# Decode attention over a long cache: VectorE passes PE's marks to the load queue by event instructions, and two loops are loaded at other slots

## The chip, the cores and the metric

The kernel runs on one core of one Trainium2 chip. The metric is the device time of one execution in microseconds (us), the median of three runs. Engines are PE (TensorE, matmul), VectorE (DVE), ScalarE (ACT), GpSimd (POOL) and SyncE (SP, which here only issues DMAs).

## The reference

One token's hidden vector `x` (512 numbers) goes through a layer norm. On the result run, side by side, an attention block with a cache and a small two-layer network; both are added to `x`.

```python
xn = _layernorm(x)
q = (xn @ wq).reshape(1, 1, 32, 128).transpose(0, 2, 1, 3)      # 32 query heads of 128
k, v = repeat(k_cache, 4), repeat(v_cache, 4)                   # 8 key/value heads, 65536 keys each
scores = einsum("bhqd,bhkd->bhqk", q, k) * 128 ** -0.5
o = einsum("bhqk,bhkd->bhqd", softmax(scores), v)
out = x + o.reshape(1, 1, 4096) @ wo + maximum(xn @ w1, 0) @ w2
```

All numbers are float32. The caches k and v hold 8 x 65536 x 128 numbers each: 268 MB for k, the same for v, read once.

## The kernel before, in words

Each of the 8 key/value heads is cut into five blocks (`PART = [7, 7, 6, 6, 6]`, in units of 2048 keys, here called tiles). That makes 40 steps (`STEPS`). There is one buffer for k (`ks`) and one for v (`vs`), each as large as the largest block, 7 tiles. A load of a block of 7 tiles is 7168 KB, of 6 tiles 6144 KB. SP issues them in turn: k, v, k, v, and so on (lines 152 to 161). Before each k load it waits until the semaphore `k_free` has counted the steps so far, before each v load the same of `v_free`. After the last step it waits for `k_free` once more, and then loads `w1` and `w2` into `ks` and `wo` into another buffer (lines 162 to 166 and 268 to 283).

A step runs as follows.

- PE (loop at line 300) waits for the k load and multiplies each of `MOST` = 7 tiles of `ks` with the current queries, four matmuls a tile (line 307). The results go in turn to two PSUM buffers, `pa` and `pb`, two tiles each. After each pair of tiles, and after the last single one, PE adds one to the semaphore `s_tiles`: it reaches 1, 2, 3 and 4 in a step. PE always works on 7 tiles; in a block of 6 the last is old data that is not used.
- VectorE (loop at line 332, one iteration a head, five blocks written out in it) waits for each mark of `s_tiles` and transposes the pair into `tr` (line 336). Then it takes 4 off `s_tiles` (line 342). A `drain` (line 343) waits until its work so far is done, and adds one to `k_free`. Then come the maximum over the block (lines 345 to 348), with PE's help the maximum over partitions (lines 350 to 353), and the bias for the exponential.
- ScalarE (loop at line 377) takes the exponentials into `wt` (line 384) and the factor `alpha` by which older sums shrink (line 390).
- PE waits for the v load, multiplies `wt` with `vs` in 56 matmuls (line 323) and adds one to `s_o`.
- VectorE waits for `s_o` and merges PE's result into `acc` (line 357 in a head's first block, line 360 in the others). The instruction that merges adds one to `v_free` when it is done.

GpSimd (lines 286 to 297) copies the next head's queries to `qcur` when `k_free` says that the last block of the head has been read. After the loops come the small network, the sums over heads and the output projection (lines 400 to 472).

The argument `head_slot` of a loop (lines 300, 332 and 377) names, for an engine, the instruction slot at which the loop's first instruction is loaded. PE's, VectorE's and ScalarE's loops all have 0. In the built program VectorE's loop has 93 instructions and ScalarE's 34.

Of the kernel before, what the change touches and what calls it, by code (L numbers as in the profile page):

```python
# [13 lines left out]
ENG = mybir.EngineType  # L14
# [3 lines left out]
HQ, HKV, DH = 32, 8, 128  # L18
# [10 lines left out]
PART = [7, 7, 6, 6, 6]  # L29
MOST = max(PART)  # L30
NP = len(PART)
# [37 lines left out]
def attention_and_mlp_kernel(  # L69
# [22 lines left out]
    nc = tc.nc  # L92
    scale = float(DH) ** -0.5
    te, ve, se, ge, sy = nc.tensor, nc.vector, nc.scalar, nc.gpsimd, nc.sync
# [35 lines left out]
    acc_o, acc_z, acc_y, pm = (ps.tile([P, 512], F32, name=n) for n in ("acc_o", "acc_z", "acc_y", "pm"))  # L130

    names = "k_in v_in tiles scores m_out bias_out a_out w_out o_out k_free v_free q_in d_out f_out f_free"
    with tc.tile_critical():
# [18 lines left out]
        for i in range(STEPS):  # L152
            h, n = divmod(i, NP)
# [69 lines left out]
        s = DV.mark  # L223
# [76 lines left out]
        with nc.Fori(0, STEPS, engines=[ENG.PE], head_slot={ENG.PE: 0}):  # L300
            te.wait_ge(k_in, 16).then_inc(k_in, -16)
            te.wait_ge(q_in, 1).then_inc(q_in, -1)  # L302
            for s in range(MOST):
                pt = (pa, pb)[s // 2 % 2][:, s % 2, :]
                for c in range(CT):
                    at = (s * CT + c) * TW
                    i = te.matmul(pt[32 * c : 32 * c + 32, :], qcur, ks[:, at : at + TW], start=True, stop=True)  # L307
# [12 lines left out]
            n = MOST * SUB // WIDE  # L320
# [8 lines left out]
            mm.then_inc(s_o, 1)  # L329


        with nc.Fori(0, HKV, engines=[ENG.DVE], head_slot={ENG.DVE: 0}):
            for n, nt in enumerate(PART):
                for s in range(0, MOST, 2):
                    w = min(2, MOST - s)
                    i = ve.transpose(  # L336
                        tr[:, s * SUB : (s + w) * SUB, :].rearrange("p b i -> p (b i)"),
                        (pa, pb)[s // 2 % 2][:, :w, :].rearrange("p i k -> p (i k)"),
                    )._wait_ge(s_tiles, s // 2 + 1)
                    if s < 4:  # L340
                        i.then_inc(s_dve, 1)
                ve.sem_inc(s_tiles, -4)
                ve.drain().then_inc(k_free, 1)  # L343
                top = m if n == 0 else mc
                i = ve.reduce_max(top, tr[:, : nt * SUB, :G].rearrange("p b g -> p g b"), axis=AX.X)  # L345
                if n:
                    ve.drain()
                    i = ve.tensor_max(m, m, mc)  # L348
                i.then_inc(s_dve, 1)
                ve.reduce_max(mg, pm[:G, :P], axis=AX.X)._wait_ge(s_max, 1)  # L350
                ve.drain()
                ve.tensor_scalar(dg, idg, mg, -scale, op0=ALU.mult, op1=ALU.mult).then_inc(s_dve, 1)  # L352
                ve.tensor_copy(bias[:, n, :], pm[:, P : P + G + 1])._wait_ge(s_max, 2).then_inc(s_bias, 1)  # L353
                ve.sem_inc(s_max, -2)
                flat = acc.rearrange("p b d -> p (b d)")
                if n == 0:
                    i = ve.tensor_copy(flat, acc_o)  # L357
                else:
                    ve.wait_ge(s_alpha, 1).then_inc(s_alpha, -1)
                    i = ve.scalar_tensor_tensor(  # L360
                        flat, flat, alpha[:, n : n + 1], acc_o, op0=ALU.mult, op1=ALU.add
                    )
                i._wait_ge(s_o, 1).then_inc(v_free, 1)
                ve.sem_inc(s_o, -1)
            ve.drain()
            last = bias[:, NP - 1, :G].unsqueeze(1).to_broadcast([P, NP - 1, G])
            ve.tensor_sub(diff, last, bias[:, : NP - 1, :G]).then_inc(s_diff, 1)
            ve.tensor_mul(masked, acc, selb.unsqueeze(2).to_broadcast([P, WIDE, DH]))
            ve.wait_ge(s_alpha, 1).then_inc(s_alpha, -1)
            ve.tensor_mul(part[:, : NP - 1, :], part[:, : NP - 1, :], fac)  # L370
            ve.wait_ge(f_free, 1).then_inc(f_free, -1)
            ve.drain()
            ve.reduce_sum(fin[:, DH:], part.rearrange("p n g -> p g n"), axis=AX.X)
            ve.reduce_sum(fin[:, :DH], masked.rearrange("p b d -> p d b"), axis=AX.X).then_inc(f_out, 1)


        with nc.Fori(0, HKV, engines=[ENG.Activation], head_slot={ENG.Activation: 0}):
            for n, nt in enumerate(PART):
                se.wait_ge(s_bias, 1).then_inc(s_bias, -1)  # L379
                if n and nt < PART[n - 1]:  # L380
                    b = slice(nt * SUB, PART[n - 1] * SUB)
                    se.copy(wt[:, b, :].rearrange("p b g -> p (b g)"), zero)  # L382
                for g in range(G):
                    i = se.activation(  # L384
                        wt[:, : nt * SUB, g], tr[:, : nt * SUB, g], AF.Exp, bias=bias[:, n, g : g + 1],
                        scale=scale, accum_out=part[:, n, g : g + 1],
                    )
                i.then_inc(s_w, 1)
                if n:
                    se.activation(  # L390
                        alpha[:, n : n + 1], bias[:, n - 1, G : G + 1], AF.Exp,
                        bias=bias[:, n, G : G + 1], scale=-1.0,
                    ).then_inc(s_alpha, 1)
            se.wait_ge(s_diff, 1).then_inc(s_diff, -1)
            se.activation(
                fac.rearrange("p n g -> p (n g)"), diff.rearrange("p n g -> p (n g)"), AF.Exp
            ).then_inc(s_alpha, 1)
# [104 lines left out]
```

## Time and profile before

| what | value |
|---|---|
| three runs | 1307.83, 1311.38, 1313.49 us; median 1311.38 |
| the profiled execution | 1308.58 us, its span (first to last instruction) 1306.8 us |
| granted PE clock, mean | 0.735 of full speed |
| busy share of the span | PE 57%, VectorE 23%, ScalarE 7% |
| read from HBM | 560.99 MB, 429 GB/s over the span |
| PE, k matmuls (line 307) | 359.4 us busy in 2240 instructions |
| PE, v matmuls (line 323) | 328.5 us busy in 2240 instructions |
| VectorE, transposes (line 336) | 176.9 us busy, 1.25 us each for a pair of tiles |
| k load of 6 tiles, issue to landing | median 19.8 us |
| v load of 6 tiles, issue to landing | median 19.4 us |

The profile comes from one execution; all durations below are its own. A landing is told by 16 marks, one from each DMA engine, as each load is cut into equal parts for the 16 engines. An instruction packet is a DMA by which an engine's program is brought in; they have queues of their own.

### The profile page before, as it was taken

The page shows a single profiled execution, that of the slowest core. Times are in us where ns is not written, and L with a number is a line of the kernel's source. Part 1 is how long each engine was busy: PE and PEld are TensorE (multiplying, and loading weights), DVE is VectorE, ACT ScalarE, POOL GpSimd, SP SyncE. Part 2 cuts the span into 40 slices and gives each one's busy share as a digit, 9 for nine tenths or more (in the row PEclk, how much of TensorE's full clock was granted, in tenths as well). Part 3 has the DMA queues.
Part 4 walks back from the last instruction along what each step waited for, and adds up shares of the span by engine and source line. Part 5 has one row for each costly group of instructions (what it writes and reads, how often), then busy time and mean ns, then how long its engine had stood idle before and what let it go on. Part 6 is the DMA issues. An engine that isn't in the chain of part 4 may idle for free. (4 is left out here: it accounts for less than half of the span.)

```text
span 1306.8 us, 11612 instructions
## 1 busy us (share of the span) xinstructions
PE 748.4 (57%) x4958; PEld 214.8 (16%) x4958; DVE 294.9 (23%) x474; ACT 88.3 (7%) x372; POOL 4.6 (0%) x22
## 2 busy tenths in 40 slices
PE   4456555556555655556655655556655656555666
PEld 1111111111111111111111111111111111111112
DVE  2122222222212222222222222222221232222221
ACT  0000000000000001000000000000000000100000
POOL 0000000000000000000000000000000000000000
PEclk9667777777767777777766777777766777777778
DMA  9999999999999999999999999999999999999998
GB/s 397 446 427 412 429 433 437 430 427 432 433 435 432 432 436 432 435 429 433 428 441 432 433 433 428 441 425 433 433 435 441 425 433 437 429 442 429 432 425 353
DMA packets 14408, 561.09 MB, mean 429 GB/s; under 512 B 1592, under 2 KB 1600, under 8 KB 1984
## 3 DMA queue, kind: packets, MB, share of 16 engines
q1 hardware_dynamic: 14248, 561.00, 99.6%
q8 instruction: 3, 0.05, 0.0%
q14 instruction: 5, 0.04, 0.0%
q10 hardware_dynamic: 152, 0.00, 0.0%
HBM read 560.99 MB, written 0.00 MB: 429 GB/s over the span
## 5 line engine op out<-in xcount | busy, mean ns | idle before, releaser
L323 PE MATMUL acc_o<-vs,wt 128*16 128x512 f32 x2240 | 328.5, 750 | 128.6 <-PEq L319 128.6
L307 PE MATMUL pa<-ks,qcur 128*32 128x512 f32 x1280 | 220.1, 820 | 285.8 <-PEq L302 285.8
L336 DVE STREAM_TRANSPOSE tr<-pa 128x1024 f32<-128x1024 f32 x80 | 100.0, 1250 | 404.2 <-PE pa L307 404.2
L307 PE MATMUL pb<-ks,qcur 128*32 128x512 f32 x960 | 139.3, 685 | 0.0
L323 PEld LDWEIGHTS acc_o<-vs,wt 128*16 128x16 f32 x2240 | 76.4, 114 | 347.2 <-issue 347.2
L384 ACT ACTIVATE wt<-tr,bias 128x96 f32<-128x96 f32 (+1 forms) x160 | 73.1, 465 | 875.5 <-ACTq L379 875.5
L307 PEld LDWEIGHTS pa<-ks,qcur 128*32 128x32 f32 x1280 | 48.6, 134 | 420.0 <-issue 409.1
L360 DVE SCALAR_TENSOR_TENSOR acc<-acc,alpha,acc_o 128x512 f32<-128x512 f32 x32 | 23.9, 747 | 348.8 <-PE acc_o L323 348.8
L336 DVE STREAM_TRANSPOSE tr<-pb 128x1024 f32<-128x1024 f32 x80 | 76.9, 962 | 38.0 <-PE pb L307 38.0
L312 PE MATMUL pm<-ident,m 128*4 128x128 f32 x40 | 11.5, 286 | 90.0 <-DVE m L348 73.0
L307 PEld LDWEIGHTS pb<-ks,qcur 128*32 128x32 f32 x960 | 41.2, 138 | 110.5 <-issue 86.6
L313 PE MATMUL pm<-dg,ones 4*128 4x4 f32 x80 | 21.6, 338 | 26.7 <-DVE dg L352 26.7
L384 ACT ACTIVATION_READ_ACCUMULATOR wt<-tr,bias 128x1 f32 x160 | 29.9, 187 | 0.0
L357 DVE COPY acc<-acc_o 128x512 f32<-128x512 f32 x8 | 5.5, 691 | 102.9 <-PE acc_o L323 102.9
L345 DVE TENSOR_REDUCE mc<-tr 128x4 f32<-128x384 f32 (+1 forms) x32 | 26.2, 819 | 3.7
L312 PEld LDWEIGHTS pm<-ident,m 128*4 128x4 f32 x40 | 3.3, 81 | 126.3 <-DVE m L348 102.0
L313 PEld LDWEIGHTS pm<-dg,ones 4*128 4x128 f32 x80 | 18.1, 280 | 34.9 <-DVE dg L352 34.9
L314 PE MATMUL pm<-dg,rowg 4*128 4x1 f32 x80 | 21.6, 337 | 0.0
L314 PEld LDWEIGHTS pm<-dg,rowg 4*128 4x128 f32 x80 | 20.6, 313 | 0.0
L382 ACT COPY wt<-zero 128x64 f32<-128x64 f32 x8 | 2.0, 244 | 232.5 <-ACTq L379 232.5
L242 PE MATMUL pa<-big,xn 128*1 128x512 f32 x64 | 11.5, 888 | 10.0 <-DMA big<-wq 10.0
L353 DVE COPY bias<-pm 128x5 f32<-128x5 f32 x40 | 6.5, 164 | 41.5 <-PE pm L314 41.5
(83 smaller groups left out, 115.3 us busy)
## 6 DMA issues: line engine op xcount, KB each, us to landing
ks<-k SPq DMA_DIRECT2D x24, 6144.0 KB, 19.8
vs<-v SPq DMA_DIRECT2D x24, 6144.0 KB, 19.4
ks<-k SPq DMA_DIRECT2D x16, 7168.0 KB, 23.5
vs<-v SPq DMA_DIRECT2D x16, 7168.0 KB, 24.3
big<-wq SPq DMA_DIRECT2D x2, 4096.0 KB, 17.2
ks<-w SPq DMA_DIRECT2D x2, 3584.0 KB, 17.7
big<-wo SPq DMA_DIRECT2D x1, 4096.0 KB, 31.4
big<-wo SPq DMA_DIRECT2D x1, 2048.0 KB, 35.9
```

The source lines that it names most:

```text
L242: lambda e: e.matmul(pr[32 * c : 32 * c + 1, :n], xn[:, a : a + 1], weights(c, a), start=(a == 0), stop=(a == A - 1),),
L307: i = te.matmul(pt[32 * c : 32 * c + 32, :], qcur, ks[:, at : at + TW], start=True, stop=True)
L312: te.transpose(pm[:G, :P], m, ident)._wait_ge(s_dve, 3).then_inc(s_max, 1)
L313: te.matmul(pm[:, P : P + G], ones[:G, :], dg[:, :G], start=True, stop=True)._wait_ge(s_dve, 4)
L314: te.matmul(pm[:, P + G : P + G + 1], rowg, dg[:, G : G + 1], start=True, stop=True).then_inc(s_max, 1)
L323: mm = te.matmul(acc_o[32 * c : 32 * c + WIDE * G, :], wt[:, i * WIDE : (i + 1) * WIDE, :].rearrange("p b g -> p (b g)"), vs[:, i * 512 : ...
L336: i = ve.transpose(tr[:, s * SUB : (s + w) * SUB, :].rearrange("p b i -> p (b i)"), (pa, pb)[s // 2 % 2][:, :w, :].rearrange("p i k -> p ( ...
L345: i = ve.reduce_max(top, tr[:, : nt * SUB, :G].rearrange("p b g -> p g b"), axis=AX.X)
L353: ve.tensor_copy(bias[:, n, :], pm[:, P : P + G + 1])._wait_ge(s_max, 2).then_inc(s_bias, 1)
L357: i = ve.tensor_copy(flat, acc_o)
L360: i = ve.scalar_tensor_tensor(flat, flat, alpha[:, n : n + 1], acc_o, op0=ALU.mult, op1=ALU.add)
L384: i = se.activation(wt[:, : nt * SUB, g], tr[:, : nt * SUB, g], AF.Exp, bias=bias[:, n, g : g + 1], scale=scale, accum_out=part[:, n, g : ...
```

## The change

Three edits.

- `k_free` no longer goes up with the drain behind all four transposes. VectorE's program instead has an event instruction that waits for a mark of `s_tiles` and adds one to `k_free`. Which mark depends on how many tiles the next k load will overwrite (`follow`). If the next block has 7 tiles, it is the fourth mark, and the event stands ahead of the last transpose. If the next has 6 tiles, it is the third mark, and the event stands right behind the third transpose. The drain stays, without the addition.
- `v_free` no longer goes up when the merge into `acc` is done. An event instruction ahead of the merge waits for `s_o` and adds one to `v_free`. The wait for `s_alpha` stands ahead of it; the merge itself waits for nothing more.
- The loop of VectorE is loaded from slot 128 and that of ScalarE from slot 68. PE's stays at 0. VectorE's loop now has 103 instructions.

```diff
-        with nc.Fori(0, HKV, engines=[ENG.DVE], head_slot={ENG.DVE: 0}):
+        with nc.Fori(0, HKV, engines=[ENG.DVE], head_slot={ENG.DVE: 128}):
             for n, nt in enumerate(PART):
+
+                follow = PART[(n + 1) % NP]
                 for s in range(0, MOST, 2):
                     w = min(2, MOST - s)
+                    if s < follow <= s + 2 and follow == MOST:
+                        ve.wait_ge(s_tiles, s // 2 + 1).then_inc(k_free, 1)
                     i = ve.transpose(
...
                     if s < 4:
                         i.then_inc(s_dve, 1)
+                    if s < follow <= s + 2 and follow < MOST:
+                        ve.wait_ge(s_tiles, s // 2 + 1).then_inc(k_free, 1)
                 ve.sem_inc(s_tiles, -4)
-                ve.drain().then_inc(k_free, 1)
+                ve.drain()
...
                 flat = acc.rearrange("p b d -> p (b d)")
+                if n:
+                    ve.wait_ge(s_alpha, 1).then_inc(s_alpha, -1)
+                ve.wait_ge(s_o, 1).then_inc(v_free, 1)
                 if n == 0:
-                    i = ve.tensor_copy(flat, acc_o)
+                    ve.tensor_copy(flat, acc_o)
                 else:
-                    ve.wait_ge(s_alpha, 1).then_inc(s_alpha, -1)
-                    i = ve.scalar_tensor_tensor(
+                    ve.scalar_tensor_tensor(
                         flat, flat, alpha[:, n : n + 1], acc_o, op0=ALU.mult, op1=ALU.add
                     )
-                i._wait_ge(s_o, 1).then_inc(v_free, 1)
                 ve.sem_inc(s_o, -1)
...
-        with nc.Fori(0, HKV, engines=[ENG.Activation], head_slot={ENG.Activation: 0}):
+        with nc.Fori(0, HKV, engines=[ENG.Activation], head_slot={ENG.Activation: 68}):
```

## The prediction

> **What bounds the kernel now.** I read the DMA queues first, because the page's slices give the DMA engines a 9 in nearly every slice while PE stands at 5. Then I read the load queue's own waits, one block of the timeline, four stretches, and the trace's records of single DMA packets and landing marks.
>
> From the page of the kernel before (queue: packets, MB, share of the 16 engines' span):
>
> ```profile
> ## 3 DMA queue, kind: packets, MB, share of 16 engines
> q1 hardware_dynamic: 14248, 561.00, 99.6%
> q8 instruction: 3, 0.05, 0.0%
> q14 instruction: 5, 0.04, 0.0%
> ```
>
> The one queue that carries k and v fills the DMA engines for 99.6% of the span. Keep the eight instruction packets in mind; they return below.
>
> What the load queue waits for (total us, times, longest):
>
> ```profile
> SPq L158 <- DVEq L343: 632.4, 39, 49.0
> SPq L161 <- DVE acc L360: 454.0, 31, 16.4
> SPq L161 <- DVE acc L357: 130.6, 8, 16.3
> ```
>
> SP stands in these waits for 1217 of 1306.8 us, and all are on VectorE, as the change supposes. But SP is only the issuer: while it waits for one buffer, the other buffer's load is still in the queue. That shows in a block of the timeline (start, duration):
>
> ```profile
> 329.36 1.04 PE L307 MATMUL pb<-ks,qcur 128*32 128x512 f32 x8
> 329.61 1.25 DVE L336 STREAM_TRANSPOSE tr<-pa 128x1024 f32<-128x1024 f32 x1 [0.47 <-PE pa L307]
> 330.79 0.67 DVE L336 STREAM_TRANSPOSE tr<-pb 128x512 f32<-128x512 f32 x1
> 331.51 0.33 SPq L158 DMA_DIRECT2D ks<-k  x1
> ...
> 344.92 0.75 DVE L360 SCALAR_TENSOR_TENSOR acc<-acc,alpha,acc_o 128x512 f32<-128x512 f32 x1 [10.11 <-PE acc_o L323]
> 345.69 0.33 SPq L161 DMA_DIRECT2D vs<-v  x1
> ```
>
> The k load of 331.51 is issued while v is still moving: v's 16 landing marks come at 334.52 to 335.94. The v load of 345.69 finds k in flight until 351.48. I call the time from an issue to the other load's first mark the **lead**: 3.0 and 5.8 us here; over the 78 issues after the first pair the median is 3.9, the smallest 2.05. In steady state a transfer of 6 tiles lands every 14.53 us, one of 7 every 16.95, whichever engine is how late.
>
> The exceptions are few (stretch, its us, busy us of each engine, granted clock, DMA share, GB/s):
>
> ```profile
> core 0: us, PE busy (x) PEld busy (x) DVE busy (x) ACT busy (x) POOL busy (x), PEclk, DMA share, GB/s
> 23.40:42.45 19.05, 5.65 (x36) 1.27 (x36) 0.86 (x2) 0.00 (x0) 0.19 (x1) 0.68 1.00 427
> 104.00:124.00 20.00, 10.48 (x69) 3.56 (x73) 5.96 (x9) 2.20 (x10) 0.00 (x0) 0.69 0.99 413
> 147.00:165.00 18.00, 9.18 (x61) 2.90 (x61) 2.51 (x7) 2.05 (x9) 0.00 (x0) 0.75 1.00 423
> 500.00:1000.00 500.00, 283.82 (x1872) 81.09 (x1872) 114.84 (x175) 34.18 (x147) 1.74 (x7) 0.72 1.00 433
> ```
>
> 433 GB/s is the plateau; the stretches at 104 and 147 lie below it. There the leads were short (2.45 and 2.61, then 2.05 us), and packets of 49152 bytes, 1.82 us each elsewhere, took up to 3.7. Long packets of the later k and v loads sit nearly all at leads under 2.8 us, which 8 of the 78 issues have. So a queue fed too late costs something, but seldom.
>
> [...]
>
> **The change part by part.**
>
> 1. *k_free.* Before, it goes up with the drain behind the last transpose (331.50). After, an event instruction sends it. Event instructions do not wait for VectorE's running work: the one of line 342 ran at 330.49, inside the transpose of 329.61 to 330.86, and took 0.02 us. For a next load of 7 tiles (2 of 5 blocks) the signal goes with PE's last pair, marked at 330.45: 1.0 us earlier. For one of 6 tiles (3 of 5) it goes with the third pair, marked at 329.59 in this block: 1.85 us earlier. If an event did wait for the transpose, the latter would be 0.6 us.
>
> 2. *v_free.* Today it goes up when the 0.75 us of line 360 end, after the change when PE's mark arrives (344.89): 0.77 us earlier.
>
> 3. *What that is worth.* On the plateau nothing: the earlier load only waits longer in its queue. At the short leads, the 2.05 becomes about 3.9 and the 2.45 about 3.2, above 2.8. What those stalls cost the end is not their packet time summed over engines but what the latest engine's mark lost: 0.06, 0.10 and 0.26 us at steps 2 to 4, nothing clear later. I take **-0.4**, between 0 and -0.65 (the last with all shortfalls of transfer rates counted).
>
> 4. *Ten more event instructions a head on VectorE,* 80 x 0.02 = 1.7 us over 1300, 0.04 a block. Behind them wait a transpose, or the merge of acc; both already wait for the same mark. Cover is the lead of 3.9 us; without it, 1.7 us. SP's issues number the same, nothing is moved past another in its queue, and GpSimd's wait for k_free at a head's end is met 1.0 us earlier. I take 0.
>
> 5. *The slots.* No time of a loop shows before's slots, but the packets do. VectorE's copy of line 262 ends at 30.33 and releases PE, ACT and itself into their loops. At 35.25, 35.27 and 35.33 an instruction packet (8192, 16384, 8192 bytes) goes in ahead of load packets, at 41.16 and 43.16 two more of 8192. The load packets right behind took 3.36, 3.27, 2.60, 2.49 and 2.78 us where 2.12 is usual. Of wq's 16 marks all lie within 0.45 us. Of v's first load, 13 lie within 0.45, the others at 1.62, 2.39 and 2.55. So fetches made three DMA engines late, and every load is cut evenly over 16, so its last mark is that of the latest. The 16384-byte packet with what follows it costs 1.126 + 0.48 = 1.61: that is the mark at 1.62. I take it for PE's, whose slot stays, because its queue and size differ from the rest. The two pairs of 8192 I put to ACT and VectorE, whose heads move from slot 0 to 68 and 128. [...] If both pairs go, the latest mark falls from 2.55 to 1.62: **-0.9**. Bounds: 0 if either pair stays on its engine, and +1.6 if one fetch more hits the latest engine (0.33 + 1.24, the dearest of the 8192). I take -0.9, since all rows fit it.
>
> [...]
>
> 6. *The tail.* PE's fetch at 1287.81 makes one engine late by 1.1 + 0.46 us. In before it hit the engine that led: the spread of marks stayed at 1.3. Where it hits after the change is unknown: 0 to +1.5, as PE's engine of 35.27 may be the latest then. I take 0, as in before.
>
> Sum: the profiled execution took 1308.58 (span 1306.8, 1.8 around it); 1308.58 - 0.9 - 0.4 = **1307.3 us**. The three runs shown are 1307.83, 1311.38 and 1313.49: the profile stands with the lowest, 2.8 below the median. The forecast says that after the change the median, too, lies near the floor. That holds if the excess of the higher runs comes from short leads, as when PE's phases last longer: a k phase now takes 8.9 to 10.5 us from landing to next issue, against a pace of 14.53.
>
> **The rivals.**
>
> - *The queue is never empty, so no wait that goes was on the path, and the higher runs have another cause* (slower packets, say). For it: the plateau of 433 over 500 us, 70 of 78 leads above 2.8. Then the median moves by at most the sum: 1311.4 - 1.3 = 1310.1, up to 1311.4. Chance 0.30.
> - *Slower: the moved loop is fetched again at each of its back edges.* Place: VectorE's loop, now 103 instructions from slot 128. If its start and end do not stay loaded together, seven back edges each put 8192 bytes ahead of loads on one DMA engine, 1.56 us each by the dearest row: 10.9 us of lateness, 1308.2 + 10.9 = 1319.1. It passes 1317.9 (0.5% over the median) only when all seven are fetched again. [...] Chance 0.06, and 0.02 for anything else that slows.
> - *It does not do what it says:* the event waits for the running transpose. Signals come 0.6 us earlier at most; the slots are left: about 1307.7. Chance 0.05.
> - *Faster than a half per cent:* all engines even and no stall. The packets at their usual durations sum to 1295.3 us an engine; with 2.1 ahead, 4.4 behind and 1.8 outside, 1303.6. Chance 0.07.
> - The forecast, 1306.0 to 1309.0: 0.50.
>
> **How the numbers follow.** A measurement of this kernel can tell about 0.5% from no change, which is 6.6 us. Faster is 0.07, slower 0.08, the rest 0.85. From 1305.0 to 1312.5 the range holds the forecast, the first rival and the third, 0.85 together less some of their tails; the unknown fetches (+1.6, +1.5) stay inside.
>
> **What would show it.** In the profile after: leads of at least 3 us; no slice but the first and the last under 425 GB/s (one of 412 before); two or fewer instruction packets on q14 before 100 us; the first k load's marks within 1.7 us; SP's waits as long in total as now, put down to other lines. Wrong, if the early fetches are all there (then 1308.2), or if q14 counts seven more (the slower rival). If issues come earlier and the median stays at 1311, the first rival holds.

## The result, and the profile after

The changed kernel takes 1307.9 us (median of 11 runs, 1306.8 to 1309.1), the kernel before 1310.05 us in the same measurement (11 runs, 1307.8 to 1313.7). The ratio is 0.9979, with a 95% interval of 0.9969 to 0.9988: 2.7 us gained, 1.6 to 4.1 by the interval; the two medians lie 2.15 us apart. Not only the median fell; the runs scatter over 2.3 us instead of 5.9 (those of the kernel before in the three later sets over 3.2, 3.3 and 6.3). The same kernel in a later set of runs, named `change_again` below, gave 0.9988 (0.9978 to 0.9997). Half a per cent, which was set as the bound to "no change", is not reached. The ratios leave out two runs far off the others of their kernel, one of before at 1349.12 us (beside `change_again`) and one of `split_loads` at 2223.9 us.

The profiled execution of the change took 1309.12 us (span 1307.2), the slowest of its 11 runs, while that of before, with 1308.58, lies below 10 of the 11 runs of before. Two single executions therefore do not show the gain as a difference of spans. It has to be read inside them.

The instruction queues on the page after (queue: packets, MB, share of the 16 engines' span):

```profile
q1 hardware_dynamic: 14248, 561.00, 99.5%
q8 instruction: 3, 0.05, 0.0%
q14 instruction: 4, 0.03, 0.0%
```

One packet fewer than before on q14 within the span. The trace's packets say which: of 35.25, 35.33, 41.16 and 43.16 us before, 35.13, 35.32 and 43.45 are still there. The slots took one fetch away and not four.

What the load queue waits for, after (total us, times, longest):

```profile
SPq L161 <- DVEq L364: 617.4, 39, 17.5
SPq L158 <- DVEq L347: 338.4, 24, 15.8
SPq L158 <- DVEq L339: 259.4, 15, 47.0
```

The waits add up to 1215.2 us, where they were 1217.0. They have only gone over to the new event instructions: line 364 for v, 347 for a next load of 6 tiles (24 times), 339 for one of 7 (15 times). A reader who expected a shorter wait would think that nothing had happened. The wait did not shrink, as the loads set the pace (q1 took 99.5% of the 16 engines' span, 99.6% before). What moved is when, within the pace, an issue falls. The block of the timeline that the prediction showed, now (start, duration):

```profile
328.61 1.25 DVE L340 STREAM_TRANSPOSE tr<-pa 128x1024 f32<-128x1024 f32 x1 [0.47 <-PE pa L307]
329.51 0.33 SPq L158 DMA_DIRECT2D ks<-k  x1
...
329.78 0.67 DVE L340 STREAM_TRANSPOSE tr<-pb 128x512 f32<-128x512 f32 x1
...
343.68 0.33 SPq L161 DMA_DIRECT2D vs<-v  x1
343.74 0.75 DVE L368 SCALAR_TENSOR_TENSOR acc<-acc,alpha,acc_o 128x512 f32<-128x512 f32 x1 [9.98 <-PE acc_o L323]
```

The k load goes out 0.90 us after the start of the third transpose, within that transpose, where it was 1.90 us: 1.0 us earlier, as worked out. That is a load of 7 tiles. The 24 loads of 6 tiles go out 0.06 us after that start, the 15 of 7 tiles 0.91, where all 39 did so at 1.90 before: 1.84 and 1.0 us earlier. The v load goes out 0.06 us ahead of the merge and not 0.77 us behind its start: 0.83 us earlier. From a load's last mark to the next issue into its buffer the medians went from 9.75 to 8.20 us (k) and from 9.70 to 8.91 (v).

The same stretches as before:

```profile
core 0: us, PE busy (x) PEld busy (x) DVE busy (x) ACT busy (x) POOL busy (x), PEclk, DMA share, GB/s
23.40:42.45 19.05, 6.35 (x40) 1.66 (x44) 0.87 (x2) 0.00 (x0) 0.19 (x1) 0.63 1.00 426
104.00:124.00 20.00, 10.53 (x65) 3.37 (x69) 5.97 (x9) 2.20 (x10) 0.00 (x0) 0.67 1.00 433
147.00:165.00 18.00, 8.87 (x61) 2.79 (x61) 1.71 (x6) 2.05 (x9) 0.00 (x0) 0.71 0.99 426
500.00:1000.00 500.00, 285.39 (x1872) 81.51 (x1872) 115.57 (x177) 34.17 (x147) 1.73 (x7) 0.72 1.00 433
```

The plateau is the same 433 GB/s: nothing was gained there, as the prediction had it. The stretch of the early fetches has 426 for 427. The one at 104 us rose from 413 to 433. The one at 147 us is a warning: the kernel without slots, below, shows 423 there and has not one long packet in it. A stretch of 18 us counts some ten starts of packets an engine, at 1.82 us each, so it can be off by a few per cent: slots_only, below, shows 437 GB/s there at a DMA share of 1.02. The durations of single packets are the better witness.

### The profile page after: what moved, and what is told of

Its sections match the earlier page's. It is cut to its first block, busy times and chain, and to the rows that moved or that the text cites. A ratio compares the mean times of both kernels' runs of the same rounds, so it can differ in the third digit from the quotient of the medians.

```text
span 1307.2 us, 11692 instructions
## 1 busy us (share of the span) xinstructions
PE 741.8 (57%) x4958; PEld 214.3 (16%) x4958; DVE 295.0 (23%) x474; ACT 88.3 (7%) x372; POOL 4.5 (0%) x22
## 3 DMA queue, kind: packets, MB, share of 16 engines
q1 hardware_dynamic: 14248, 561.00, 99.5%
## 5 line engine op out<-in xcount | busy, mean ns | idle before, releaser
L307 PE MATMUL pb<-ks,qcur 128*32 128x512 f32 x960 | 135.7, 669 | 0.0
## 6 DMA issues: line engine op xcount, KB each, us to landing
big<-wq SPq DMA_DIRECT2D x2, 4096.0 KB, 17.3
```

## The experiments

Twelve kernels ran, in three sets of four; each set shared one chip and the runs of the kernel before on it. In the table a load's marks are its 16 landing marks; "long" are packets of 49152 or 57344 bytes between 60 and 1270 us that took at least 0.02 us more than usual (1.82 and 2.12 us). Times of marks are of one profiled execution each, in us; the median and the ratio are of 5 to 11 runs.

| kernel | median, ratio (interval) | first v load, last mark | last v load: mean, last mark | long packets | last load of all, last mark |
|---|---|---|---|---|---|
| before | 1310.05 | 59.41 | 1265.28, 1265.79 | 84 | 1302.91 |
| the change | 1307.90, 0.9979 (0.9969 to 0.9988) | 59.40 | 1263.91, 1265.14 | 67 | 1302.66 |
| change_again | 1308.04, 0.9988 (0.9978 to 0.9997) | 59.40 | 1263.73, 1265.16 | 41 | 1302.08 |
| slots_only | 1309.46, 1.0001 (0.9992 to 1.0010) | 59.50 | 1265.50, 1266.08 | 153 | 1304.59 |
| signals_only | 1308.49, 0.9989 (0.9980 to 0.9998) | 59.87 | 1264.29, 1265.69 | 67 | 1302.61 |
| signals_again | 1308.97, 0.9991 (0.9982 to 1.0001) | 59.61 | 1264.11, 1265.50 | 61 | 1302.55 |
| k_only | 1310.12, 1.0003 (0.9994 to 1.0012) | 58.98 | 1264.19, 1265.02 | 99 | 1303.17 |
| v_only | 1310.78, 1.0008 (0.9999 to 1.0017) | 59.40 | 1265.26, 1265.93 | 79 | 1303.33 |
| later_1 | 1352.57, 1.0325 (1.0311 to 1.0339) | 59.65 | 1305.04, 1306.60 | 1242 | 1345.68 |
| later_2 | 1375.36, 1.0509 (1.0494 to 1.0523) | 59.45 | 1319.71, 1321.37 | 1216 | 1361.46 |
| no_slots_only | 1308.51, 0.9992 (0.9982 to 1.0001) | 58.48 | 1264.14, 1264.66 | 98 | 1302.86 |
| no_slots | 1307.29, 0.9980 (0.9971 to 0.9989) | 58.64 | 1263.12, 1264.56 | 5 | 1301.50 |
| no_slots_pe | 1307.27, 0.9977 (0.9968 to 0.9986) | 58.36 | 1263.08, 1264.16 | 3 | 1301.20 |

The twelfth, `split_loads`, has packets of other sizes and is told below.

### Which part of the change: slots or signals

**slots_only** is the kernel before with only this:

```diff
-        with nc.Fori(0, HKV, engines=[ENG.DVE], head_slot={ENG.DVE: 0}):
+        with nc.Fori(0, HKV, engines=[ENG.DVE], head_slot={ENG.DVE: 128}):
...
-        with nc.Fori(0, HKV, engines=[ENG.Activation], head_slot={ENG.Activation: 0}):
+        with nc.Fori(0, HKV, engines=[ENG.Activation], head_slot={ENG.Activation: 68}):
```

> The kernel before with the two loops at slots 128 and 68 and nothing else. If the fetches of instructions make the gain, the time falls by about 2 us as in the full change (ratio 0.998). If the signals make it, the ratio is 1.000 and the runs scatter as before, over 5 us. The profile of the full change still has the three early fetches, so I expect the latter, and three or four instruction packets between 30 and 50 us.

Measured: 1.0001 (0.9992 to 1.0010), and four early packets, at 33.1, 33.3, 33.3 and 39.3 us. The slots by themselves give nothing that can be seen. A gain of 0.9 us would still lie within the interval; what speaks against it is the first v load's last mark, at 59.50.

**signals_only** is the reverse: the change with both loops back at slot 0.

> Both signals early, both loops at slot 0 as before. If the signals make the gain: 2 us under the kernel before (0.998), with less scatter. If the slots make it: 1.000. The leads should be those of the full change: median about 4.8 us for k, 3.9 for v.

Measured: 0.9989 (0.9980 to 0.9998), 1.4 us at the ratio, with a scatter of 2.0 us. The signals carry the gain, or most of it, as far as intervals of 0.1% on either side can tell. The leads were as expected, 4.77 (k) and 3.87 us (v).

**k_only** keeps the new k_free at slot 0, and puts the merge of acc back as it was:

```diff
-                ve.wait_ge(s_o, 1).then_inc(v_free, 1)
...
+                i._wait_ge(s_o, 1).then_inc(v_free, 1)
```

> Only the signal for k is early. Its lead grows by 1.0 to 1.85 us. If the queue's short leads are what costs, and those of k and v count alike, about half to two thirds of the gain, 1 to 1.5 us (0.999); the v leads stay as short as before. If slots make the gain, 1.000.

**v_only** does the same for the other signal: only the merge's edit, and k_free with the drain.

> Only the signal for v is early, by 0.77 us. By the theory of short leads, the smaller part: 0.5 to 1 us (0.9995). If slots make the gain, 1.000.

Measured: 1.0003 (0.9994 to 1.0012) and 1.0008 (0.9999 to 1.0017). That was a miss. Each signal was to bring its part, and neither brought any that can be measured. The leads explain some of it. With v alone early, k's median lead fell from 3.91 to 3.40 us, and 11 issues lay under 2.8 us where 8 did. With k alone, v's fell from 3.90 to 3.70, and 4 lay under, all of them v's, where 3 of v's did. One early signal shifted its own load, and the other buffer stayed the weak place. What the long packets took beyond the usual, summed over the 16 engines, falls in steps: 30.2 us before and 38.5 in slots_only, 25.1 with v alone, 20.0 with k alone, 9.9 to 17.3 in the four profiles of the change and of signals at slot 0. Against before that is 0.3 and 0.6 us an engine for the single signals, which the intervals hardly resolve, and 0.8 to 1.3 for both. That does not settle k_only: its marks are nearly those of both signals together (1265.02), its median is not. Its profile, like that of v_only, is of the fastest of its 11 runs and so does not show the ordinary one. Even there its last load ends late: PE's fetch at 1300.78 precedes it, and its last mark, at 1303.17, stands 1.1 us behind its second last.

**change_again** and **signals_again** repeat two kernels side by side on one chip.

> The changed kernel once more, beside the one without its slots on the same chip. So far it stood at 0.998 and the signals alone at 0.999, on different chips. If slots 128 and 68 add something to the signals, it is 1 us faster than signals_again; if not, both stand at 0.998 to 0.999 within 0.5 us of each other.

> Both signals early, slots 0: 0.9985 if the slots of the change do nothing, 0.999 beside 0.998 if they do. A second profile also shows how the latest mark of the first v load varies between executions; five early packets of instructions as before.

Measured: 0.9988 (0.9978 to 0.9997) against 0.9991 (0.9982 to 1.0001), medians 1308.04 and 1308.97. The intervals lie on top of each other. Whether slots 128 and 68 add up to 1 us to the signals stays open; alone they add nothing.

### Does the lead matter at all: signals later instead of earlier

**later_1** delays the signals of the kernel before. The values computed stay the same; `masked` is overwritten before it is used.

```diff
-                ve.drain().then_inc(k_free, 1)
+                ve.drain()
...
-                ve.drain()
+                ve.drain().then_inc(k_free, 1)
                 ve.tensor_scalar(dg, idg, mg, -scale, op0=ALU.mult, op1=ALU.mult).then_inc(s_dve, 1)
...
-                i._wait_ge(s_o, 1).then_inc(v_free, 1)
+                i._wait_ge(s_o, 1)
                 ve.sem_inc(s_o, -1)
+                for _ in range(2):
+                    ve.drain()
+                    ve.memset(masked, 0.0)
+                ve.drain().then_inc(v_free, 1)
```

> The kernel before with its signals later instead of earlier: k_free 1.8 us later (with the drain of line 351), v_free about 1.2 us later (two fills of an unused tile ahead of it). Theory of short leads: the leads fall from a median of 3.9 to about 2.1 for k and 2.7 for v, most lie under 2.8, long packets become many, and the time rises by 1 to 5 us (ratio 1.001 to 1.004). Rival (the queue is never empty, signals do not matter): 1.000.

**later_2** has four fills and sends k_free behind the copy of the bias.

> As the one before, but k_free 3.3 us later (behind line 354) and v_free about 2.4 us later. Short leads: k about 0.6, v about 1.5, below 2.8 at every issue, so that even the latest DMA engine runs dry at each: up to 1 us at each of 78 issues, 10 to 60 us in all (1.01 to 1.045). Rival: 1.000.

Measured: 1.0325 (1.0311 to 1.0339) and 1.0509 (1.0494 to 1.0523), that is 42.6 and 66.7 us. The rival that the signals do not matter, because the queue is never empty, has fallen. My size for later_1 fell with it: its upper end was 5 us, an eighth of what was measured. The range for later_2 (10 to 60 us) was passed too. The leads of later_1 came out as expected, with a median of 2.03 us for k and 2.65 for v, 50 of 78 under 2.8 us; those of later_2 are longer than expected, 1.18 and 2.40, with 49 of 78 under 2.8 and not all. In later_1 each issue cost the latest mark 0.5 us on average (40.6 us more than before from the first v load's last mark to the last one's, over 78 issues). The plateau of later_1, in the view of stretches:

```profile
core 0: us, PE busy (x) PEld busy (x) DVE busy (x) ACT busy (x) POOL busy (x), PEclk, DMA share, GB/s
500.00:1000.00 500.00, 285.17 (x1816) 81.33 (x1815) 125.59 (x203) 34.26 (x148) 1.92 (x8) 0.71 0.99 418
```

and its load queue's waits:

```profile
SPq L158 <- DVEq L351: 664.1, 39, 50.5
SPq L161 <- DVEq L368: 594.2, 39, 16.2
```

The share of busy time shows only a part of the loss: 0.99 instead of 1.00, while the rate fell from 433 to 418. A packet that was held up counted as busy all the while: 1242 packets took longer than usual, together 419 us of 16 engines, 26 us each. From 60 to 1260 us the engines stood idle for a further 13 us each; the two make up nearly all of the 40.6. The fills that were added are not what costs: VectorE is busy for 125.59 of the 500 us, and its transposes into `tr` still wait 368.2 us in all for PE's `pa` (404.2 before). The waits of SP, too, grew only from 1217 to 1258 us. Rate and packet durations showed the late feeding better than the busy share did.

**split_loads** goes the other way and makes the leads long. Each load is cut at tile 4; the first part is asked for by a mark of PE's own, sent as soon as PE is through tiles 0 to 3.

```diff
+            for held, free, dst, row, at, sem in (
+                (k_half, k_free, ks, k[h, 0], lo * KEYS, k_in), (v_half, v_free, vs, flat_v, 0, v_in)
+            ):
+                for mark, x0, x1 in ((held, 0, FIRST * KEYS), (free, FIRST * KEYS, nt * KEYS)):
+                    if i:
+                        sy.wait_ge(mark, i)
+                    sy.dma_start(dst[:, x0:x1], row[:, at + x0 : at + x1]).then_inc(sem, 16)
...
+                    if c == 1 and s == FIRST:
+                        i.then_inc(k_half, 1)
...
+                if i == FIRST * SUB // WIDE:
+                    mm.then_inc(v_half, 1)
```

> The changed kernel with each load cut in two: tiles 0 to 3 are asked for as soon as PE has read them (a mark of PE's own, with no VectorE between), the rest as in the changed kernel. The leads become 6 us and more. Theory of short leads: no long packets after 60 us, the mark lost nothing; the time falls a little more, by 0 to 1 us below the changed kernel (ratio 0.997 to 0.998 to before), and the runs scatter by under 2 us. If the twice as many DMAs cost, 1 to 3 us more.

Measured: 1.0028 (1.0016 to 1.0039), median 1313.95, seven runs. Up to the first mark of the other buffer's second part, the first parts' leads have medians of 5.7 (k) and 5.6 us (v), and one packet of the k and v loads was long between 60 and 1270 us. So the stalls went, and still it was slower, by 6 us against the change, where 1 to 3 had been allowed for more DMAs. Its page:

```profile
DMA packets 25927, 561.09 MB, mean 428 GB/s; under 512 B 2872, under 2 KB 2880, under 8 KB 3264
...
q1 hardware_dynamic: 25768, 561.00, 99.7%
```

and a stretch of its plateau:

```profile
500.00:1000.00 500.00, 285.88 (x1864) 81.48 (x1860) 115.23 (x176) 34.19 (x147) 1.74 (x7) 0.72 1.00 431
```

The smaller packets carried less per us. 57344 bytes took 2.119 us, 49152 took 1.819, 32768 took 1.216, 24576 took 0.915 and 16384 took 0.614 us: the last is 427 GB/s over 16 engines, the first 433. Summed over the k and v loads that is 19972 us for the halves against 19855 whole, 7.3 us an engine. Less the 0.8 us an engine that the change's long packets cost, it is the size of the loss: the price of the halves was not in the queue but in the packets.

### What the early fetches cost

**no_slots** has both signals early and names no slot for the loops of VectorE and ScalarE; against the change:

```diff
-        with nc.Fori(0, HKV, engines=[ENG.DVE], head_slot={ENG.DVE: 128}):
+        with nc.Fori(0, HKV, engines=[ENG.DVE]):
...
-        with nc.Fori(0, HKV, engines=[ENG.Activation], head_slot={ENG.Activation: 68}):
+        with nc.Fori(0, HKV, engines=[ENG.Activation]):
```

> Both signals early, and no slot named for the loops of vector and scalar engine: they follow the code ahead of them with no branch over padding. If entering the loops by a branch makes the early fetches of 8192 bytes, those at 33 to 43 us vanish, the first v load's latest mark falls from 2.6 to about 1.6 us behind the first, and the time falls by a further 0.9 us below signals alone (0.998). If a loop then crosses a border of loaded code at each turn, one packet more per turn and 1 to 10 us slower. If the fetches have another cause, the time of signals alone (0.999).

Measured: 0.9980 (0.9971 to 0.9989), median 1307.29, runs within 1.1 us of each other. Its queues and two stretches:

```profile
q8 instruction: 3, 0.05, 0.0%
...
q14 instruction: 3, 0.02, 0.0%
```

```profile
23.40:42.45 19.05, 7.63 (x40) 1.66 (x44) 0.87 (x2) 0.00 (x0) 0.19 (x1) 0.59 1.00 431
...
147.00:165.00 18.00, 9.21 (x61) 2.70 (x61) 1.83 (x6) 2.05 (x9) 0.00 (x0) 0.74 0.98 423
```

None of the early 8192-byte packets is left; its three of q14 stand at 92, 195 and 1141 us. Of the first v load 15 marks lie within 0.35 us, and one, by the size and time of its fetch that of PE's, 1.80 behind the first. The first v load's last mark came at 58.64 instead of 59.4 to 59.9 (58.98 in k_only, whose five fetches lie further apart). The price of the fetches is about as worked out, 0.9 us; only the change's slots do not remove them. Long packets were 5.

**no_slots_only** leaves the signals as they were.

> The kernel before, its signals as they were, with no slot named for the loops of vector and scalar engine. If the early fetches and the short leads cost separately, the first v load's latest mark is 1.8 us behind the first instead of 2.6, and the time falls by 0.8 to 1 us (0.9993). If the smaller spread of marks also lengthens the leads (they count from the first mark), long packets fall as well, and the gain is larger, 1.5 to 2 us (0.9987).

Measured: 0.9992 (0.9982 to 1.0001), median 1308.51, last mark of the first v load 58.48. That is the first answer, 0.8 to 1 us, though the interval holds the other too, and no gain as well. The leads did lengthen, to medians of 4.11 (k) and 4.31 us (v), 4 of them under 2.8, but long packets stayed at 98, 22.0 us beyond the usual: even marks at the start did not replace the lead. The two remedies seem to add up: no slots alone 0.9992, signals alone 0.9989 and 0.9991, both 0.9980; each step is of the size of the intervals.

**no_slots_pe** takes PE's slot away as well, beside no_slots.

> Both signals early and no slot named on any of the three loops. If PE's branch into its loop makes the fetch of 16384 bytes at 35 us, that goes too, all 16 marks of the first v load lie within 0.5 us, and the time falls by up to 1.5 us below 1307.3 (0.997). If PE's loop then lies across a border of loaded code and is fetched again at each turn, up to 40 packets of 16384 bytes at 1.1 us and more, and 1320 us or above (1.008 and more).

Measured: 0.9977 (0.9968 to 0.9986), median 1307.27, the same as no_slots. PE's 16384-byte packet did not go but moved to 45.8 us. The marks of the first k load lie within 0.44 us, those of the first v load again 1.58 apart. PE's loop was not fetched again at its turns, which had been put at 1320 us or above. These two kernels are the fastest of all that ran; on intervals they cannot be told from the change.

## Why the prediction was right, and where it was not

**The bound, and points 1 to 3: right in kind, point 3 at its far end or beyond.** The kernel is bound by its loads, the plateau stays at 433 GB/s, the events go out while VectorE still works (1.0 and 0.83 us earlier in the block shown), and what pays are the short leads. The stall's size was put at -0.4 with ends of 0 and -0.65. Within the loop the profiles agree with the far end: from the first to the last v load's last mark it is 1206.38 us before and 1206.58 in slots_only, against 1205.74, 1205.76, 1205.82 and 1205.89 in the four profiles with both signals (slots named), so 0.5 to 0.8 us. With k alone early it is 1206.04, with v alone 1206.53. In the runs it looks like more, 1.4 and 1.2 us by the two ratios of the signals alone, but their intervals (0.3 to 2.6 us, and -0.1 to 2.4) hold 0.65 too.

I had taken what the latest mark lost as the whole price. The mean mark shows the rest: at the last v load it comes 1.0 to 1.8 us earlier with both signals (1263.7 to 1264.3 against 1265.3 and 1265.5; without the early fetches, in no_slots_only, it stands at 1264.1 with the signals of before). Short leads held up the early engines until they stood beside the latest; the spread of these marks before was 1.35 us, after it 2.2. An engine that had lost its advance had nothing left when something hit it later. PE's fetch near 1288 us did: it cost the engine it met 1.6 us (1.10 for itself, and 0.46 in the load packet behind it, 0.77 for 0.31, in before as in the change). In the profile of slots_only the first `wo` load's last mark stands at 1294.60, 1.6 us behind the second last. In signals_only that gap is 0.05, in the change 0.59, where it was 0.65 ahead of that fetch. So the engine hit in signals_only had enough advance to take it. Luck has its part: in the profile of before the gap is 0.15, in no_slots_only 1.28. That this happens more often without the early signals would fit the larger gain in the runs. It is argued from one profile of each kernel, and not shown for the ordinary runs. Nor does a wide spread alone mean that advance is left: later_1, with the shorter leads, has 2.30.

**Point 5 failed.** The term of -0.9 rested on four fetches that vanish once the heads are at 68 and 128. No run shows that: five early packets became four, in the change as in slots_only. The latest mark of the first v load stayed where it was: 59.41, then 59.40 and 59.40. The price was right, since no_slots and no_slots_only bring that mark to 58.6 and 58.5. What was wrong is that the new heads would be entered without a fetch. VectorE and ScalarE still branch into their loops, at 30.58 and 30.70 us (30.25 and 30.37 before; in no_slots VectorE has no branch there), and two packets follow at 35.13 and 35.32 as they did at 35.25 and 35.33. Why the later two became one stays open. Without point 5 the sum is 1308.2, and the measured 1307.9 lies 0.3 below it, which point 3 would give at its end of -0.65. That 1307.3 came within 0.6 us is thus in part luck: a gain that did not come, and one put too small, partly cancel. And most of the fall of the median, from 1310.05 to the 1308.58 from which the sum starts, is no term of the sum at all; it was taken over from the condition on the higher runs.

**Of point 4** nothing was seen that costs. **Point 6**, the tail, was left at 0 with an end of +1.5. It is real and varies: from the last mark of the last v load to that of the last load of all it is 37.1 us before, 38.5 in slots_only, 37.5 and 36.9 in the two profiles of the change. Behind an early landing the kernel then waited for PE. The chain that ended last in change_again, as its page sums it by engine, names no load any more (in before it was DMA 3% and PE 1%):

```profile
PE 2%; DVE 0%; issue 0%; DVEq 0%
```

The same holds of signals_only, signals_again and no_slots_pe; in the change and in no_slots the chain still runs over the load of `wo`. So a part of what the loads gain at the end is given back: the span ended 4.2 us after the last mark there, 3.9 before.

**The rivals.** That no wait that goes was on the path does not hold: the six kernels with whole loads and both signals early have ratios of 0.9977 to 0.9991, five of the six intervals end below 1, and late signals cost 42.6 us in later_1. Its other half, that the higher runs have another cause, is not ruled out: no_slots_only, with the signals of before, also has its median at 1308.51 and a scatter of only 2.5 us. That the event would wait for the transpose is refuted by the block shown. A fetch at every back edge did not occur in any kernel: in before no instruction packet goes out between 43.16 and 1143.34 us, in the change none between 43.45 and 1139.77. In no_slots one packet of 8192 bytes goes out at 194.66, 4.95 us behind VectorE's first back edge (189.71); none follows the next five turns. The forecast that the median itself would come down to the floor of the single fast runs held in the change, with the scatter; that short leads alone had lifted the higher runs is not shown.

**The signs.** Of the signs named, most failed narrowly. Leads of at least 3 us: no, the smallest were 2.59 (k) and 2.55 (v), three under 2.8. The v lead's median did not rise, 3.92 for 3.90: it counts to the first mark, and the first mark now comes earlier (1262.95 for 1264.44 at the last v load), since the early engines were held up less. No slice under 425: one of 424. Two early packets on q14: three. First k load's marks within 1.7 us: 2.0.

## What to carry to other kernels

Here one queue of loads set the pace, at 99.6% of the DMA engines' span, and two buffers alternated; the issuer's wait, 1217 of 1306.8 us, was not time lost, however long it stands in the profile. In a kernel of that kind ask how long before the other load's end the next one is issued. Here packets grew long at leads under about 3 us (71 of the 84 long ones before at leads under 2.8, 80 of the 98 in no_slots_only under 3.2), and with medians of 2.0 and 2.7 in later_1 each issue cost 0.5 us, of which the busy share shows about a third. Cutting the loads to gain lead was no remedy, as the smaller packets carried less (431 GB/s on the plateau for 433); send the signal on the mark of the instruction that reads the data last, and for both buffers, as one alone gave nothing measurable (1.0003 for k, 1.0008 for v).

## What the runs showed of the hardware that was not expected

- The busy share of the DMA engines hardly fell when loads were issued late: 0.99 of the time at 418 GB/s (later_1), 1.00 at 433 (before). Durations of packets told: a median of 1.82 us for 49152 bytes, up to 3.7 at a late issue (before).
- A DMA engine that was made late stayed late. In no_slots one mark of the first v load stands 1.80 us behind the first, after the fetch of 16384 bytes at 35.48, and one of the ninth 1.83, nearly 250 us later. In before, where short leads held up the others in between, the spread fell from 2.55 to 1.55 over the same loads.
- A fetch of 8192 bytes took 0.31 to 0.47 us by itself in the profiles of before and the change, and made its engine 0.7 to 1.9 us late, as the load packet that started when it ended, otherwise 2.12 us, took 2.5 to 3.7. The loads paid for these fetches; whether the engine that executes waited, no run here shows.
